# Batch 0's first stage in two halves of output rows, with the first weight halves in one software queue

## The chip, the cores and the metric

The kernel runs on one core of a Trainium2 chip. Its time is the device time of one execution in microseconds (us). The engines are TensorE (PE, with PEld for its weight loads), VectorE (DVE), ScalarE (ACT), GpSimd (POOL) and SyncE (SP, which here only issues transfers). POOL issues the transfers of the software queue, which here also turn float32 into bfloat16 on the way.

## What is computed

```
X = fft(fft(x, axis=1), axis=2).real      # x: 8 batches x 3072 x 256
h = max(X @ w1, X @ w2, X @ w3)           # 24576 x 768
out = h @ w_out                           # 24576 x 256
```

The two Fourier transforms and the weights w1, w2, w3 are real matrix products in the kernel. A row and its mirror row share products: of the two results hp and hm, the second is the first with one product more added.

## The kernel before

**The work of a batch** has three steps. Stage one (`Mix.s`, L531) has seven parts, k = 0 to 6, and multiplies the batch's x by small 96-row matrices (m24f, m24r, m0f, m0r); the seven results are copied from PSUM to the tile z. Stage two (`Mix.k`, L559) has six parts, each of eight products of z with rows of the sine table `tab`, copied to the tile t. Then come 18 units (`UNITS`, three blocks of six): `unit_plus` (L585) multiplies t by gE and gO into two PSUM tiles, pse2 and pse3; `unit_out` (L602) has ACT take relu of pse2 and DVE the maximum of that with pse3, which gives hp; `unit_minus` (L595) then adds gD to the same two tiles, and `unit_out` makes hm from them. pse2 and pse3 have two buffers each. The second matrix product (L616) and the stores follow.

**Preparation.** The gE, gO and gD tiles are made in `prep_first` (L472) from d2 = w2 - w1 and d3 = w3 - w1 (`differences`, L231), one half of the 768 columns at a time (jh = 0, 1), each by products with md, which holds the transform of the columns. Half 0 is made before the units, half 1 between units 0 and 2. `dif` and `sgn` are small per-partition constants. `prep_second` (L492) makes g1t and gw, for which w_out is needed.

**Batch 0's x** comes in four loads of rows of 128: rows 112 to 127 by SP and ACT into xs_a, and rows 0 to 39, 40 to 79 and 80 to 111 by POOL, four transfers each (L259). Each is laid out twice: in natural order (`lay_rows`, L418, tile nat) and reversed (`turn_rows`, L412, tile back), by copies that ACT and DVE share (L426 to L453). PE does warm-up products on the table until x is laid out (L772); then stage one takes nat and back whole.

**The order of the work** is written out by hand: each engine runs its instructions in the order in which the program issues them, and the list at L858 gives what is added after which unit of batch 0. So ACT's sines of table rows 10 to 12 stand in ACT's order at unit 2 (`tab_sines(10, 13, (0,))`); their angles come from POOL (`tab_angles(10, 13, nc.gpsimd)`, L793). `tab_minus` (L342) writes the negative of a part of the table.

**Queues.** POOL issues x, then both halves of w1 (L267). SP issues w2 and w3, half 0 and then half 1 (L269), after the first transfer of the third x load has landed, and behind them batch 1's x in four chunks (L458). After `first_op` (L460), which waits until x is laid out, POOL fills two constants, computes the row numbers of the stores (`store_rows`, L278, in the tiles rows_f and late of the pool `gen`), negates table rows 7 to 9 (L467), then forms the two differences of half 1, issues w_out's load, computes the angles of rows 10 to 12 and starts laying out batch 1 (`turn_chunk`, L149). The pool `gen` ends before the units begin, and later tiles take its memory.

Of the kernel before, what the change touches and what calls it, by code (L numbers as in the profile page):

```python
# [33 lines left out]
def kernel(  # L34
# [196 lines left out]
    def differences(eng, jh, which=(0, 1), after=None):  # L231
# [22 lines left out]

    pidx = gen.tile([128, 1], FP32, tag="pidx")
# [19 lines left out]
    rows_f = gen.tile([128, 7 * B], FP32, tag="rows_f")  # L275
    late = gen.tile([128, 1], FP32, tag="late")

# [145 lines left out]
    def bf_rows(r0, n):  # L423
        return x0_first[:, r0 * 64:(r0 + n) * 64]
# [20 lines left out]
    nc.scalar.activation(out=md[0], in_=vm, func=AX.Sin, scale=float(-2.0 * math.pi / 256.0))  # L445
    turn_rows(on_dve, 39, 40, 32, 65)
    lay_rows(on_act, bf_rows(40, 40), 40, 40, 12, 33)
    second_laid = lay_rows(on_dve, bf_rows(40, 40), 40, 40, 0, 12)
    for (copy, a, b, c, d) in ((on_act, 55, 64, 21, 33), (on_dve, 32, 55, 0, 21)):
        third_turned = turn_rows(copy, 79, 33, a, b)  # L450
        if copy is on_act:
            turn_rows(copy, 79, 32, 64, 65)
        laid = lay_rows(copy, bf_rows(80, 32), 80, 32, c, d)  # L453
    nc.vector.tensor_scalar(out=sgn, in0=pidx, scalar1=0.0, scalar2=None, op0=ALU.is_equal)
    nc.vector.tensor_scalar(out=sgn, in0=sgn, scalar1=2.0, scalar2=-1.0,
                            op0=ALU.mult, op1=ALU.add)
    nc.vector.tensor_scalar(out=dif, in0=sgn, scalar1=1.0, scalar2=None, op0=ALU.subtract)
    for ch in range(4):  # L458
        raw[1, ch] = load_chunk(1, ch)
    first_op = nc.gpsimd.memset(mark, 0.0)  # L460
    tc.add_manual_dep(first_op.ins, laid.ins.name, AFTER, reason="the two share a port")
    nc.gpsimd.memset(two_row, 0.0)
# [9 lines left out]
    def prep_first(jh, bank):  # L472

        cs = slice(jh * 384, (jh + 1) * 384)
        for i, wv in enumerate((d2_bf, d3_bf)):
            for half in range(2):
                psg = bank()
                hs = slice(half * 128, (half + 1) * 128)
                for fc in range(2):
                    nc.tensor.matmul(  # L480
                        psg[:, 0:384], md[fc][:, hs],
                        wv[:, fc * DFF + jh * 384: fc * DFF + jh * 384 + 384],
                        start=(fc == 0), stop=(fc == 1))
                if half == 0:
                    nc.vector.tensor_copy(out=gE[i][:, cs], in_=psg[:, 0:384])
                else:
                    nc.scalar.copy(out=gO[i][:, cs], in_=psg[:, 0:384])
                    nc.vector.tensor_scalar(out=gD[i][:, cs], in0=psg[:, 0:384], scalar1=dif,
                                            scalar2=None, op0=ALU.mult)
                yield  # L490
# [32 lines left out]
    class Mix:  # L523
# [6 lines left out]

        def s(self, k, x0, pool=ps_f, evict=nc.scalar.copy):  # L531

# [6 lines left out]
            for (d, n, mf, mr) in parts:  # L539
                if isinstance(x0, tuple):  # L540
                    pairs = ((x0[0](d), mf), (x0[1](d), mr))
                elif d:
                    pairs = ((x0[:, d, :], mf),)
                else:
                    pairs = ((x0[:, 0, :], mf), (x0[:, 33, :], mr))
                for i, (st, mv) in enumerate(pairs):
                    nc.tensor.matmul(ps1[:, c0:c0 + n], st, mv[:, 0:n], start=(i == 0),  # L547
                                     stop=(i == len(pairs) - 1))
                c0 += n
            if k < len(DLS):  # L550
                lo = 4 * DLS[k][0]
                evict(out=z[:, lo:lo + 20, 0:24],  # L552
                      in_=ps1[:, 0:480].rearrange("p (c r) -> p c r", r=24))
            else:
                evict(out=z_all[:, 0:52], in_=ps1[:, 0:52])
                evict(out=z[:, 2:8, 0:24],
                      in_=ps1[:, 52:196].rearrange("p (c r) -> p c r", r=24))

        def k(self, q, evict=nc.scalar.copy, pool=ps_f):  # L559
# [24 lines left out]

    def unit_plus(te, to, jc, n):  # L585
# [4 lines left out]
        for (pse, i) in ((pse2, 0), (pse3, 1)):  # L590
            nc.tensor.matmul(pse[:, 0:n], gE[i][:, js], te, start=True, stop=False)  # L591
# [179 lines left out]
    warm = ps_s.tile([128, 512], FP32, name="warm", tag="ps")  # L771
    for (n, after) in ((23, None), (3, second_laid), (2, third_turned)):  # L772
        for i in range(n):
            mm = nc.tensor.matmul(warm, tab[:, 0:128], tab[:, 0:512], start=True, stop=True)
# [3 lines left out]
    x0f = (lambda d: xn0[:, d, 0:128], rows_back(xr0))  # L778
    for k in range(7):
        m.s(k, x0f, pool=ps_s if k % 4 else ps_f,  # L780
            evict=nc.vector.tensor_copy if k in (1, 3) else nc.scalar.copy)
        if k == 1:
            halves = [t.rearrange("p (q two g) -> p two q g", two=2, g=4) for t in md]
            nc.vector.tensor_copy(out=halves[1][:, 0], in_=halves[0][:, 0])
            nc.vector.tensor_scalar(out=halves[1][:, 1], in0=halves[0][:, 1], scalar1=-1.0,
                                    scalar2=None, op0=ALU.mult)
            differences(nc.vector, 0, (0,))
        if k == 3:
            first_half = differences(nc.vector, 0, (1,))
            differences(nc.gpsimd, 1, after=first_half)  # L790
            nc.gpsimd.dma_start(out=wout_bf.rearrange("p (jc c) -> p jc c", jc=NJC),
                                in_=moe_w_out.rearrange("(jc p) c -> p jc c", jc=NJC))
# [100 lines left out]
    for b in range(B):  # L893
# [15 lines left out]
        for blk in range(3):  # L909
# [7 lines left out]
            for jc in range(NJC):  # L917
                pses = unit_plus(tE[:, cs], tO[:, cs], jc, TOKB)
                unit_out(pses, hp[:, jc, :], TOKB)
# [51 lines left out]
```

## Time and profile before

| what | value |
|---|---|
| median of 3 runs | 404.82 us (404.76 to 404.88) |
| the profiled execution | 404.64 us |
| its span in the profile | 402.9 us |
| instructions in the span | 8560 |
| granted TensorE clock, mean | 1.0 |

The span runs from the first to the last instruction of the profiled execution; the time of the execution includes what lies around it. In a timeline row the first number is the start in us from the begin of the span, the second the length in us, then the engine, line of the program, operation, output and inputs; in brackets is the idle time ahead of it and what ended that. In a row of the chain of waits there are start, length, engine, tile and line. In a row by stretch there are the stretch, its length, the busy time of PE, PEld, DVE, ACT and POOL with their numbers of instructions, the granted clock, the DMA share and GB/s.

### The profile page before, as it was taken

The numbers are of one execution on the slowest core, as the hardware profiler recorded it, in microseconds if no ns is written. First come the engines' busy times: TensorE is split into PE (matmuls) and PEld (weight loads), VectorE is DVE, ScalarE is ACT, GpSimd is POOL, SyncE is SP. The second block draws the span as 40 slices with busy tenths as digits, with TensorE's granted clock in tenths as the row PEclk, the third lists the DMA queues.
The fourth block names the chain that finished last, engine by engine and source line by source line (L and its number), as shares of the span: only waits on it lengthen the run. The fifth ranks groups of instructions, "written<-read, shape, count | busy, mean of one in ns | idle before, by whom it ended". The sixth has DMA issues, their size and how long they took to land.

```text
span 402.9 us, 8560 instructions
## 1 busy us (share of the span) xinstructions
PE 386.0 (96%) x2829; PEld 260.6 (65%) x2877; DVE 308.9 (77%) x556; ACT 265.5 (66%) x489; POOL 292.0 (72%) x394
## 2 busy tenths in 40 slices
PE   0999999999999999999999999999999999999996
PEld 0465667666676667666666666666677676666665
DVE  8898776788777877687776887787777877678884
ACT  6787767655866667756766677666766676655550
POOL 9599889879986998679877888768967524323521
PEclk9999999999999999999999999999999999999999
DMA  9989897789778838875478928886234411211214
GB/s 117 188 199 179 157 226 197 174 213 196 186 197 214 192 120 217 193 184 159 114 200 186 227 78 222 197 191 179 81 103 114 123 55 74 84 52 54 103 57 156
DMA packets 127597, 62.06 MB, mean 154 GB/s; under 512 B 111616, under 2 KB 116736, under 8 KB 126976
## 3 DMA queue, kind: packets, MB, share of 16 engines
q1 hardware_dynamic: 101976, 42.21, 42.3%
q0 software_dynamic: 24640, 18.98, 23.8%
q8 instruction: 22, 0.36, 0.4%
q10 hardware_dynamic: 936, 0.33, 0.3%
q14 instruction: 23, 0.19, 0.2%
HBM read 33.74 MB, written 29.88 MB: 158 GB/s over the span
## 4 chain that ended last, share of the span: by engine, by line
PE 85%; DVE 4%; DMA 3%; POOL 2%; ACT 2%; issue 2%; DVEq 0%; SPq 0%; POOLq 0%; ACTq 0%
PE po L616 29%; PE pse L591 16%; PE pse L599 14%; PE pse L592 12%; PE ps L571 3%; PE ps L573 3%; PE po L640 3%; PE pl L629 2%; PE ps L547 2%; POOL x L111 2%; DMA raw_w<-in_moe_w_dram 2%; DVE hm L606 2%; ACT stmp L605 2%; DMA x<-in_x_dram 2%; DVE other L643 1%
## 5 line engine op out<-in xcount | busy, mean ns | idle before, releaser
L605 ACT ACTIVATE stmp<-pse 128x512 bf16<-128x512 f32 x288 | 170.8, 600 | 52.6 <-PE pse L592 26.2
L606 DVE TENSOR_TENSOR hp<-pse,stmp 128x512 bf16<-128x512 f32 x144 | 99.5, 691 | 80.1 <-ACT stmp L605 51.8
L646 POOL TENSOR_TENSOR even<-even,other 128x256 f32<-128x256 f32 x92 | 70.1, 762 | 74.5 <-DVE other L643 74.2
L591 PE MATMUL pse<-t,gE 128*128 128x512 bf16 x288 | 109.1, 379 | 2.5
L606 DVE TENSOR_TENSOR hm<-pse,stmp 128x512 bf16<-128x512 f32 x144 | 99.2, 689 | 3.3 <-ACT stmp L605 3.1
L592 PE MATMUL pse<-t,gO 128*128 128x512 bf16 x249 | 94.3, 379 | 0.0
L616 PE MATMUL po<-wout_bf,hp 128*128 128x256 bf16 x576 | 85.9, 272 | 0.0
L616 PE MATMUL po<-wout_bf,hm 128*128 128x256 bf16 x570 | 85.3, 273 | 0.3
L599 PE MATMUL pse<-t,gD 128*128 128x512 bf16 x279 | 83.7, 379 | 0.1
L677 POOL DMA_INDIRECT out_dram<-ot,rows_m x53 | 53.8, 1015 | 20.2 <-DVE ot L670 10.7
L616 PEld LDWEIGHTS <-hp 128*128 128x128 bf16 x576 | 56.3, 98 | 17.3 <-issue 2.5
L616 PEld LDWEIGHTS <-hm 128*128 128x128 bf16 x576 | 56.4, 98 | 16.5
L670 DVE TENSOR_TENSOR ot<-po,even 128x512 f32<-128x512 f32 x92 | 62.8, 682 | 0.0
L173 POOL CAST xw<-xs 96x544 bf16<-96x544 f32 (+1 forms) x48 | 53.2, 1120 | 0.0
L178 POOL CAST xb<-xs 96x512 bf16<-96x512 f32 x48 | 52.4, 1100 | 0.0
L575 ACT CAST t<-ps 128x512 bf16<-128x512 f32 x48 | 27.9, 585 | 34.8 <-PE ps L573 34.7
L599 PEld LDWEIGHTS <-gD 128*128 128x128 bf16 x288 | 28.1, 98 | 32.2
L643 DVE SCALAR_TENSOR_TENSOR other<-twice,po 128x256 f32<-128x256 f32 x92 | 43.8, 476 | 0.1
L592 PEld LDWEIGHTS <-gO 128*128 128x128 bf16 x288 | 28.1, 98 | 20.4 <-issue 1.9
L591 PEld LDWEIGHTS <-gE 128*128 128x128 bf16 x288 | 28.2, 98 | 19.5 <-issue 0.7
L552 ACT CAST z_all<-ps 128x480 bf16<-128x480 f32 x46 | 24.8, 560 | 22.0 <-PE ps L547 21.9
L632 ACT COPY even<-pl 128x512 f32<-128x512 f32 x46 | 27.0, 587 | 9.7 <-PE pl L629 8.6
(178 smaller groups left out, 370.9 us busy)
## 6 DMA issues: line engine op xcount, KB each, us to landing
xs<-in_x_dram SPq DMA_DIRECT2D x84, 198.0 KB
out_dram<-ot SPq DMA_DIRECT2D x39, 256.0 KB
xs<-in_x_dram SPq DMA_DIRECT2D x28, 192.0 KB
held<-xb SPq DMA_DIRECT2D x48, 96.0 KB
xw<-held POOLq DMA_DIRECT2D x24, 192.0 KB
raw_w<-in_moe_w_dram SPq DMA_DIRECT2D x4, 384.0 KB
out_dram<-ot SPq DMA_DIRECT2D x12, 128.0 KB
x<-in_x_dram POOLq DMA_DIRECT2D x8, 120.0 KB
```

The costliest lines, as they stand in the source:

```text
L173: nc.gpsimd.tensor_copy(v[:, d0:d1, ch * 32:ch * 32 + 32], xs[:, 0:32 * 64].rearrange("p (bb dl) -> p dl bb", dl=64)[:, d0:d1, :])
L178: nc.gpsimd.tensor_copy(mir[:, d0:d1, c0:c0 + 32], bass.AP(xs.tensor, xs.offset + 33 * 64 - 1 - d0, [xs.ap[0], [-1, d1 - d0], [-64, 32]]))
L591: nc.tensor.matmul(pse[:, 0:n], gE[i][:, js], te, start=True, stop=False)
L592: nc.tensor.matmul(pse[:, 0:n], gO[i][:, js], to, start=False, stop=True)
L599: nc.tensor.matmul(pse, gD[i][:, js], to, start=False, stop=True, skip_group_check=True)
L605: nc.scalar.activation(out=stmp[:, 0:n], in_=pses[0][:, 0:n], func=AX.Relu)
L606: nc.vector.tensor_tensor(out=dst, in0=src3, in1=stmp[:, 0:n], op=ALU.max)
L616: nc.tensor.matmul(po, hcols(jc), wout_bf[:, jc * 256:(jc + 1) * 256], start=False, stop=(jc == NJC - 1), skip_group_check=True)
L643: nc.vector.scalar_tensor_tensor(out=other, in0=twice, scalar=po[:, 256:257], in1=po[:, 0:256], op0=ALU.mult, op1=ALU.subtract)
L646: nc.gpsimd.tensor_tensor(out=line[:, 256:512], in0=line[:, 0:256], in1=other, op=ALU.add)
L670: nc.vector.tensor_tensor(out=parts, in0=po.rearrange("p (i c) -> p i c", i=2), in1=lin.rearrange("p (i c) -> p i c", i=2), op=ALU.add)
L677: stored(nc.gpsimd.indirect_dma_start(out.rearrange("(n two) c -> n (two c)", two=2) if pair else out, bass.IndirectOffsetOnAxis(ap=rows_m ...
```

## The change

Stage one of batch 0 is done in two halves of z's 128 output rows. The first half (`sooner`) takes rows 0 to 63 of nat and their mirror rows of back, the second (`later`) the others; each product has 64 columns of weights and writes 64 partitions, and both halves add into seven PSUM tiles that are held at once. The copies to z follow part by part in the second half. The second x load is rows 40 to 83 and the third rows 84 to 111, so that the first half needs the first two alone. The warm-up products are 20 before the first half and one between the halves.

The first halves of w1, w3 and w2 and the second half of w1 are loaded by POOL's queue, in this order; SP loads the second halves of w3 and w2. The order of w2 and w3 is swapped in `prep_first` and in the first `unit_plus` as well. The first difference of half 0 (w3) goes from DVE to POOL, with sgn and dif. The copies within md are made before the third x load is laid out. The row numbers, pidx and late get memory that lasts (`whole`), and `store_rows` and `tab_minus(7, 10)` are issued after the differences of half 1.

```diff
+    whole = consts.tile([128, 64], FP32, tag="whole")
+    rows_f, pidx, late = whole[:, 0:7 * B], whole[:, 56:57], whole[:, 57:58]
...
-    for (r0, r1) in ((0, 40), (40, 80), (80, 112)):
+    for (r0, r1) in ((0, 40), (40, 84), (84, 112)):
...
-    for jh in range(2):
-        load_w(nc.gpsimd, w1_bf, moe_w1, jh)
-    for jh in range(2):
-        for wsrc, wdst in zip((moe_w2, moe_w3), raw_w):
-            ld = load_w(nc.sync, wdst, wsrc, jh)
-            if jh == 0:
-                tc.add_manual_dep(ld.ins, last_part[0].ins.name, AFTER, reason="x first")
+    load_w(nc.gpsimd, w1_bf, moe_w1, 0)
+    load_w(nc.gpsimd, raw_w[1], moe_w3, 0)
+    load_w(nc.gpsimd, raw_w[0], moe_w2, 0)
+    load_w(nc.gpsimd, w1_bf, moe_w1, 1)
+    for (wsrc, wdst) in ((moe_w3, raw_w[1]), (moe_w2, raw_w[0])):
+        ld = load_w(nc.sync, wdst, wsrc, 1)
+        tc.add_manual_dep(ld.ins, last_part[0].ins.name, AFTER, reason="x first")
...
-    nc.vector.tensor_scalar(out=sgn, in0=pidx, scalar1=0.0, scalar2=None, op0=ALU.is_equal)
...
+    def sooner(d):
+        return xn0[:, d, 0:64], (xr0[:, 32 - d, 64:128] if d else xr0[:, 32, 65:129])
+
+    def later(d):
+        return xn0[:, d, 64:128], (xr0[:, 32 - d, 0:64] if d else xr0[:, 32, 1:65])
...
-    nc.gpsimd.memset(two_row, 0.0)
-    nc.gpsimd.memset(two_row[0:1], 2.0)
-    nc.gpsimd.memset(gw[:, 512:513], 0.0)
-    nc.gpsimd.memset(gw[0:1, 512:513], 1.0)
-    store_rows()
-    tab_minus(7, 10, nc.gpsimd)
...
+        def s_half(self, k, rows, ps1):
+
+            begin = rows is sooner
+            if k < len(DLS):
+                parts = [(d, 96, m24f, m24r) for d in range(*DLS[k])]
+            else:
+                parts = [(0, 52, m0f, m0r), (32, 48, m24f, m24r), (1, 96, m24f, m24r)]
+            c0 = 0
+            for i, (d, n, mf, mr) in enumerate(parts):
+                for j, (st, mv) in enumerate(zip(rows(d), (mf, mr))):
+                    p0 = 64 * j if begin else 64 - 64 * j
+                    nc.tensor.matmul(ps1[p0:p0 + 64, c0:c0 + n], st, mv[:, 0:n],
+                                     start=begin and i == 0,
+                                     stop=not begin and i == len(parts) - 1,
+                                     skip_group_check=True)
+                c0 += n
...
-    for (n, after) in ((23, None), (3, second_laid), (2, third_turned)):
...
+    warm_up(20)
     m = Mix(0)
...
     for k in range(7):
-        m.s(k, x0f, pool=ps_s if k % 4 else ps_f,
-            evict=nc.vector.tensor_copy if k in (1, 3) else nc.scalar.copy)
+        m.s_half(k, sooner, banks_s[k])
+    warm_up(1, third_turned)
+    for k in range(7):
+        m.s_half(k, later, banks_s[k])
+        m.s_out(k, banks_s[k], nc.vector.tensor_copy if k % 2 else nc.scalar.copy)
         if k == 1:
...
-            differences(nc.vector, 0, (0,))
-        if k == 3:
-            first_half = differences(nc.vector, 0, (1,))
-            differences(nc.gpsimd, 1, after=first_half)
-            nc.gpsimd.dma_start(out=wout_bf.rearrange("p (jc c) -> p jc c", jc=NJC),
-                                in_=moe_w_out.rearrange("(jc p) c -> p jc c", jc=NJC))
-            tab_angles(10, 13, nc.gpsimd)
-    slots = [ps_s, ps_s, ps_f, ps_f]
+            differences(nc.gpsimd, 0, (1,))
+            nc.gpsimd.tensor_scalar(out=sgn, in0=pidx, scalar1=0.0, scalar2=None,
+                                    op0=ALU.is_equal)
...
+            nc.gpsimd.memset(two_row, 0.0)
+            nc.gpsimd.memset(two_row[0:1], 2.0)
+            nc.gpsimd.memset(gw[:, 512:513], 0.0)
+            nc.gpsimd.memset(gw[0:1, 512:513], 1.0)
+    first_half = differences(nc.vector, 0, (0,))
+    differences(nc.gpsimd, 1, (1, 0), after=first_half)
+    store_rows()
+    tab_minus(7, 10, nc.gpsimd)
+    nc.gpsimd.dma_start(out=wout_bf.rearrange("p (jc c) -> p jc c", jc=NJC),
+                        in_=moe_w_out.rearrange("(jc p) c -> p jc c", jc=NJC))
+    tab_angles(10, 13, nc.gpsimd)
+    slots = [ps_s, ps_f, ps_s, ps_f]
```

In the changed program the line numbers behind these places are up to 38 higher.

More of the change, by code (lines that the diff above doesn't have):

```diff
@@ L445 @@
     nc.scalar.activation(out=md[0], in_=vm, func=AX.Sin, scale=float(-2.0 * math.pi / 256.0))
-    turn_rows(on_dve, 39, 40, 32, 65)
-    lay_rows(on_act, bf_rows(40, 40), 40, 40, 12, 33)
-    second_laid = lay_rows(on_dve, bf_rows(40, 40), 40, 40, 0, 12)
+    turn_rows(on_dve, 39, 44, 32, 65)
+    lay_rows(on_act, bf_rows(40, 44), 40, 44, 12, 33)
+    lay_rows(on_dve, bf_rows(40, 44), 40, 44, 0, 12)
+    halves = [t.rearrange("p (q two g) -> p two q g", two=2, g=4) for t in md]
+    nc.vector.tensor_copy(out=halves[1][:, 0], in_=halves[0][:, 0])
+    nc.vector.tensor_scalar(out=halves[1][:, 1], in0=halves[0][:, 1], scalar1=-1.0,
+                            scalar2=None, op0=ALU.mult)
     for (copy, a, b, c, d) in ((on_act, 55, 64, 21, 33), (on_dve, 32, 55, 0, 21)):
-        third_turned = turn_rows(copy, 79, 33, a, b)
+        third_turned = turn_rows(copy, 83, 29, a, b)
         if copy is on_act:
[L452 to L457, printed above, removed]
+            turn_rows(copy, 83, 28, 64, 65)
+        laid = lay_rows(copy, bf_rows(84, 28), 84, 28, c, d)
+    def sooner(d):
+        return xn0[:, d, 0:64], (xr0[:, 32 - d, 64:128] if d else xr0[:, 32, 65:129])
+    def later(d):
+        return xn0[:, d, 64:128], (xr0[:, 32 - d, 0:64] if d else xr0[:, 32, 1:65])
     for ch in range(4):
@@ L487, in prep_first @@
                     nc.scalar.copy(out=gO[i][:, cs], in_=psg[:, 0:384])
-                    nc.vector.tensor_scalar(out=gD[i][:, cs], in0=psg[:, 0:384], scalar1=dif,
-                                            scalar2=None, op0=ALU.mult)
+                    scaled.append((gD[i][:, cs], psg[:, 0:384]))
+                if half and (jh or not i):
+                    for (dst, product) in scaled:
+                        nc.vector.tensor_scalar(out=dst, in0=product, scalar1=dif,
+                                                scalar2=None, op0=ALU.mult)
+                    scaled = []
                 yield
```

28 lines of the change are left out of this document (15 added, 13 removed).

## The prediction

> **What bounds the kernel now.** I read the page from the top first: busy time, then the chain that ended last.
>
> ```profile
> span 402.9 us, 8560 instructions
> PE 386.0 (96%) x2829; PEld 260.6 (65%) x2877; DVE 308.9 (77%) x556; ACT 265.5 (66%) x489; POOL 292.0 (72%) x394
> ...
> PE 85%; DVE 4%; DMA 3%; POOL 2%; ACT 2%; issue 2%; DVEq 0%; SPq 0%; POOLq 0%; ACTq 0%
> ```
>
> PE is busy for 96% of the span and holds 85% of the chain. Then the busy time by stretch, to see where PE is not the limit:
>
> ```profile
> 0.00:18.67 18.67, 8.33 (x29) 3.12 (x29) 15.87 (x58) 14.31 (x23) 13.55 (x22) 1.00 1.73 137
> ...
> 24.18:33.18 9.00, 8.70 (x47) 4.75 (x48) 8.01 (x15) 7.93 (x16) 8.80 (x8) 1.00 0.91 164
> ...
> 40.00:400.00 360.00, 356.98 (x2633) 244.18 (x2676) 274.83 (x466) 234.21 (x432) 258.28 (x350) 1.00 0.60 152
> ```
>
> From 40 to 400 us PE lacks 3 us of being always busy, so a delay that PE enters that stretch with is not made up there: what happens before 40 us reaches the end one for one, up or down. Up to 18.67 PE's work is only warm-up. Between 24.18 and 33.18 POOL is busy 8.80 of 9.00 us: POOL, not PE, is the fullest engine there. The chain of waits says the same:
>
> ```profile
> 2.63 6.14 POOL x L111 x7
> 8.76 6.22 DMA x<-in_x_dram
> ...
> 15.98 7.10 DMA raw_w<-in_moe_w_dram
> ...
> 23.25 1.65 POOL d_bf L233
> ...
> 31.98 0.45 PE pst L499 x4
> ...
> 33.18 0.38 PE pse L591
> 33.56 0.22 PE pse L592
> ```
>
> So batch 0's x, then the weights w2 and w3, then POOL's differences set the start.
>
> **The change, part by part.** First stage one. The timeline of PE, then of DVE, ACT:
>
> ```profile
> 10.01 7.73 PE L774 MATMUL warm<-tab 128*128 128x512 bf16 x26 [10.01 <-DVE tab L343]
> ...
> 18.67 0.20 PE L547 MATMUL ps<-m24f,nat 96*128 96x96 bf16 x1
> 18.71 0.20 PE L547 MATMUL ps<-m24r,back 96*128 96x96 bf16 x1
> ...
> 21.36 0.20 PE L547 MATMUL ps<-m24r,back 96*128 96x96 bf16 x1
> ...
> 14.23 1.33 DVE L144 COPY back<-x 96x1320 bf16<-96x1320 bf16 x1
> 15.48 0.58 DVE L419 COPY nat<-x 96x480 bf16<-96x480 bf16 x1
> 17.03 0.83 DVE L144 COPY back<-x 96x759 bf16<-96x759 bf16 x1 [0.97 <-DMA x<-in_x_dram]
> 17.78 0.74 DVE L419 COPY nat<-x 96x672 bf16<-96x672 bf16 x1
> ...
> 17.77 0.85 ACT L419 COPY nat<-x 96x384 bf16<-96x384 bf16 x1
> 21.99 0.31 ACT L556 CAST z_all<-ps 128x144 bf16<-128x144 f32 x1
> ```
>
> The first half of stage one needs rows 0 to 63, that is the first two loads. The second load grows from 40 to 44 rows, so DVE's two copies of it grow by 1.1: 14.23 + 1.25 x 1.1 + 0.58 x 1.1 = 16.25; with an estimated 0.3 us by which a load with a tenth more in it lands later, 16.55. The third shrinks to 28 or 29 rows: 17.03 + 0.75 x 0.88 + 0.65 = 18.35, and ACT's share ends near 18.45. So the second half can begin at 18.4, where all of stage one began at 18.67.
>
> What a half costs is not in the trace. Stage one's 66 matmuls now start about 0.042 us apart, the first at 18.67 and the last at 21.36: 2.7 us. A half has 66 too, each writing 64 partitions instead of 128. If two neighbours, which write different partitions, run beside each other, a half takes 1.4; if not, 2.7. No row is nearer to one than to the other; I take 2.1, and keep both ends. The Trainium skill, TensorEngine Tiling (Array Packing), "Theoretical Speedup", has two-way column tiling up to twice as fast, which would be the 1.4; its "Restrictions" say that column tiling switches off fast weight load, which speaks against this change; no run here shows either, and the sum below does not hang on it.
>
> With 2.1 the first half is 16.55 to 18.65, the one warm-up 0.22, the second half 18.9 to 21.0, and z is copied out by about 21.6 (DVE now takes three of seven copies, ACT four), where it was 22.30. With 1.4 it is 20.9. The copies of md move into DVE's idle 0.97 us ahead of 17.03 and cost nothing there (without that cover 0.2 us). sgn and dif leave DVE, the first d3 difference too. Fewer warm-ups cost nothing: 20 of them end before 16.55.
>
> Now the weights and POOL. POOL's timeline:
>
> ```profile
> 12.94 1.48 POOL L263 DMA_DIRECT2D w_bf<-in_moe_w_dram  x2
> 18.59 0.09 POOL L460 MEMSET mark<- 1x1 f32 x1 [4.17 <-DVE sgn L454]
> 18.62 0.20 POOL L462 MEMSET two_row<- 128x128 bf16 x1
> ...
> 19.22 0.45 POOL L245 IOTA rows_f<- 128x40 f32 x3
> 19.75 0.27 POOL L283 TENSOR_SCALAR late<-pidx 128x1 f32<-128x1 f32 x1
> 20.11 0.35 POOL L285 TENSOR_SCALAR rows_f<-rows_f,late 128x8 f32<-128x8 f32 x1
> ...
> 21.52 1.19 POOL L343 TENSOR_SCALAR tab<-tab 128x384 bf16<-128x384 bf16 x1
> 23.25 3.24 POOL L233 TENSOR_TENSOR d_bf<-raw_w,w_bf 128x768 bf16<-128x768 f32 x2 [0.54 <-DMA raw_w<-in_moe_w_dram]
> 26.44 0.91 POOL L791 DMA_DIRECT2D wout_bf<-in_moe_w_out_dram  x1
> 27.37 0.85 POOL L319 TENSOR_TENSOR w_late<-pi_all,step 128x384 f32<-128x384 f32 x1
> ...
> 29.57 1.00 POOL L329 TENSOR_TENSOR w_late<-w_high,w_late 128x384 f32<-128x384 f32 x1
> 30.52 2.04 POOL L158 CAST x<-xs 96x1056 bf16<-96x1056 f32 x1
> ```
>
> Two more weight loads are issued by POOL, 0.74 us each: 14.42 becomes 15.9, inside POOL's 4.17 us of idle time ahead of the mark, so nothing. SP issues two fewer, so batch 1's chunks start about 1 us sooner behind them.
>
> Before, POOL laid out the row numbers (19.22 to 21.52, 2.30 us) and tab_minus (to 22.75, 1.23 us) **while it waited** for w2 and w3. The change puts both behind the two second-half differences, and puts in their place the first d3 difference (1.64), three tiny operations for sgn and dif (0.36 each by the starts at 19.75 and 20.11, 1.1) and the four memsets (0.6). From the mark at 18.4 these end at 21.8. That is the earliest for the second-half differences; the latest is their start of before, 23.25, since the same six loads share the same engines. Which load lands last in the new order no row shows (w1's second half is now the last of its queue); I take the middle, 22.5. Then:
>
> 22.5 + 3.2 (both differences) + 2.30 + 1.23 + 0.93 (w_out's issue) + 3.2 (the angles of rows 10 to 12, 27.37 to 30.57) = 33.35, where it was 30.57. With the bounds: 32.65 to 34.1.
>
> Who waits for these angles? ACT's sines of rows 10 to 12, in unit 2 of batch 0, whose place in ACT's order is unchanged:
>
> ```profile
> 30.24 0.59 ACT L575 CAST t<-ps 128x512 bf16<-128x512 f32 x1
> 30.72 0.53 ACT L335 ACTIVATE tab<-w_late 128x384 bf16<-128x384 f32 x1
> 31.15 1.26 ACT L605 ACTIVATE stmp<-pse 128x512 bf16<-128x512 f32 x2
> ...
> 31.77 0.69 DVE L606 TENSOR_TENSOR hp<-pse,stmp 128x512 bf16<-128x512 f32 x1 [0.26 <-PE pse L599]
> 32.44 0.69 DVE L606 TENSOR_TENSOR hm<-pse,stmp 128x512 bf16<-128x512 f32 x1
> ```
>
> Before, the angles were ready at 30.57 and ACT came to them at 30.72: it just fitted. Now ACT comes about 0.9 us sooner (first differences of the second half done at 22.5 + 1.6 = 24.1 instead of 24.90, and z sooner) and **stands until 33.4**. Queued behind the sine on ACT are unit 3's two outputs (31.15), behind them DVE's two (31.77, 32.44), and behind those PE's unit 4 at 33.18, as the buffers come free only then. So PE's 33.18 becomes 33.18 + (33.45 - 30.72) = 35.9: **2.75 us later**, whatever was gained ahead of it; POOL's chunk of batch 1 moves from 30.52 to 33.3, the same amount, so nothing catches up. d3's first difference starts no later than POOL's chain allows and adds nothing more.
>
> w_out is issued 2.8 us later, and PE's use of it moves as far: nothing. d2's difference on DVE ends by about 22.6, beside 22.5 on POOL. The swapped order of w3 and w2, the later gD and the other banks only shift work within the gain that ACT then waits away: nothing, with at most 0.3 either way. Row numbers in memory of their own take no time; they let the row numbers be written late.
>
> Sum: 404.64 us (the profiled execution: span 402.9 and 1.7 around it; 0.2 under the median of 404.82) + 2.75 = **407.4**. Bounds by POOL's start alone: +2.1 to +3.5, 406.7 to 408.1.
>
> **The rivals.**
>
> 1. The gain of stage one reaches the end (403.7). Mechanism: POOL's row numbers and tab_minus shrink, because at 19 to 22 us they ran beside DVE's differences, and the angles are done when ACT arrives. Price: -0.9. It decides only if POOL ends them by 29.8, 3.5 us sooner than worked out. Against: the operations from 18.4 on add up to 32.65 with no wait at all. For: spans on POOL are rough.
>
> 2. Halves one matmul at a time: 2.7 each. First half to 19.25, second 19.5 to 22.2, z at 22.75, DVE's difference of d2 at 23.7, for which POOL's second-half differences wait: 1.2 us behind 22.5, so 408.6. The turning point is a half of 2.1 us. For: the matmuls of 18.67 start one after another; against: they all write the same partitions.
>
> 3. The clock falls. PE's last work ahead of unit 4 ended at 32.43 and would end near 31.5; unit 4's first buffer comes free when ACT's pair at 31.15 has ended, 32.41 + 2.75 = 35.15: a pause of 3.6 us. The first 26 warm-ups took 7.73 us, where 26 at the 0.22 of the row at 33.56 take 5.7: a cold start costs 2.0 us. If the pause were long enough, 409.4. Against: the stretches above all have the clock at 1.00; for: none of them has a pause like it. The Trainium skill, TensorE: Matmul & The Clock Gate, "Why this matters for your kernels" counts gaps of over about 3 us between bursts of matmuls as enough to go back to half clock; the pause worked out here stands just above it, and no run here yet has such a gap.
>
> 4. The change doesn't do what it says: the one queue brings w1's second half later than 23.25, for instance at 24.2. Then every microsecond of it comes on top: 408.5.
>
> **How the numbers follow.** Forecast (406.4 to 408.1) 0.58; rival 1 0.12; rival 2 0.07; rival 3 0.10; rival 4 0.06; a pause partly taken back by PE, within 0.2% (what a measurement of this kernel can tell from no change), 0.05; slower by less than the forecast's low end 0.02. The range 405.6 to 409.6 leaves out rival 1, the unchanged case (0.17 together) and little above. Faster 0.12, same 0.05, slower 0.83.
>
> **What would show it.** In the changed profile: (a) stage one's matmuls begin near 16.55, z's last copy ends before 22; (b) POOL's second-half differences begin between 21.8 and 23.25 and the angles end near 33.3; (c) ACT's sine after unit 2 shows an idle time of 3 to 4 us ended by POOL's w_late; (d) PE has one gap of 3 to 4 us there, and the rest of the run is the old one, 2.7 us later; (e) the clock stays at 1.00. The forecast is wrong if (c) shows no wait: then rival 1. It is too low if the first-half matmuls stay 0.042 apart for 2.7 us, or the clock row drops behind the gap.

## The result, and the profile after

| | before | changed |
|---|---|---|
| median, us | 404.79 (404.41 to 405.21, 6 executions) | 410.40 (407.98 to 410.95, 6 executions) |
| ratio | | 1.0131 (95% interval 1.0106 to 1.0156) |
| profiled execution, us | 404.64 | 410.13 |
| its span, us | 402.9 | 408.3 |
| granted clock, mean | 1.0 | 0.996 |

The change costs 5.6 us. The forecast was 407.4 with a range up to 409.6: the sign was right, the size half of what came. Five executions had a granted clock of 0.996 and took 410.11 to 410.95 us; the one at 1.0 took 407.98.

The page of the changed kernel: span, busy time, shares of the chain that ended last.

```profile
span 408.3 us, 8675 instructions
...
PE 385.6 (94%) x2887; PEld 260.6 (64%) x2936; DVE 308.2 (75%) x553; ACT 265.1 (65%) x488; POOL 295.9 (72%) x400
...
PE 83%; DVE 5%; POOL 4%; ACT 3%; issue 2%; DMA 2%; DVEq 0%; ACTq 0%; POOLq 0%
```

PE is as busy as before (386.0 us then) in a span that is 5.4 us longer, so it waits more; POOL and ACT have gained shares of the chain. The same stretches as in the prediction, and the one between, show where (after each engine's busy time come the clock, the share of the DMA engines and GB/s):

```profile
24.18:33.18 9.00, 7.33 (x43) 4.17 (x42) 5.97 (x10) 5.25 (x10) 8.50 (x14) 1.00 0.87 170
33.18:40.00 6.82, 3.92 (x15) 2.29 (x16) 3.27 (x5) 4.19 (x8) 6.82 (x5) 0.76 0.91 165
40.00:400.00 360.00, 356.98 (x2619) 242.94 (x2664) 275.86 (x468) 237.49 (x438) 262.27 (x352) 1.00 0.59 150
```

From 40 to 400 us PE is busy for 356.98 us, as before. Nearly all of the loss is made by 40 us: PE loses 1.37 us of work between 24.18 and 33.18, and in the 6.82 us behind that it works for 3.92 (6.60 before), part of them at half clock. Now the steps, in order. Stage one's first half, its end, the second half (PE), and the last copies of z (ACT, DVE):

```profile
16.71 0.23 PE L578 MATMUL ps<-m24f,nat 96*64 96x96 bf16 x1 [1.05 <-DVE nat L417]
16.72 0.23 PE L578 MATMUL ps<-m24r,back 96*64 96x96 bf16 x1
...
18.08 0.21 PE L578 MATMUL ps<-m24r,back 96*64 96x96 bf16 x1
18.54 0.23 PE L578 MATMUL ps<-m24f,nat 96*64 96x96 bf16 x1 [0.25 <-issue]
...
19.90 0.21 PE L578 MATMUL ps<-m24r,back 96*64 96x96 bf16 x1
...
20.43 0.32 ACT L564 CAST z_all<-ps 128x144 bf16<-128x144 f32 x1
```

The two matmuls of a pair start 0.00 to 0.01 us apart, the pairs 0.042: a half takes 1.37 us from its first start to its last, and z is out by 21 us instead of 22.3. This part did what it says. The Trainium skill, TensorEngine Tiling (Array Packing), "Theoretical Speedup", has two column tiles up to twice as fast; the trace agrees, as 66 products of half the width take 1.37 us instead of 2.7. Its "Restrictions" name the loss of fast weight load; what that costs, no run here shows by itself.

POOL, and the transfers that were issued between 14 and 24.5 us (the last number is the time from issue to landing):

```profile
18.39 1.65 POOL L233 TENSOR_TENSOR d_bf<-raw_w,w_bf 128x768 bf16<-128x768 f32 x1
...
21.32 0.09 POOL L824 MEMSET gw<- 1x1 bf16 x1
23.85 3.24 POOL L233 TENSOR_TENSOR d_bf<-raw_w,w_bf 128x768 bf16<-128x768 f32 x2 [2.44 <-DVE gD L491]
27.05 0.46 POOL L247 IOTA whole<- 128x40 f32 x3
27.58 0.24 POOL L281 TENSOR_SCALAR whole<-whole 128x1 f32<-128x1 f32 x1
...
28.54 0.23 POOL L286 CAST rows_m<-whole 128x56 int32<-128x56 f32 x1
28.74 1.20 POOL L341 TENSOR_SCALAR tab<-tab 128x384 bf16<-128x384 bf16 x1
...
33.04 0.99 POOL L327 TENSOR_TENSOR w_late<-w_high,w_late 128x384 f32<-128x384 f32 x1
```

```profile
w_bf<-in_moe_w_dram POOLq DMA_DIRECT2D x1, 192.0 KB, 8.7
```

POOL is done with its small work at 21.4 and then stands for 2.44 us. The row names a DVE operation, which ended at 23.65 by the chain of waits, but the transfer of w1's second half, issued at 15.00, took 8.7 us to land: 23.7. It is the fourth weight load in its queue. The DVE operation that the program makes POOL wait for, d2's difference, had ended by 21.9, so the transfer is what is left; run 10's trace names it. Then the chain runs without a break and the angles end at 34.03. ACT's sine, and PE's units around it:

```profile
25.54 0.81 PE L480 MATMUL psg<-d_bf,md_all 128*128 128x384 bf16 x4 [1.33 <-POOL d_bf L233]
...
34.07 0.52 ACT L333 ACTIVATE tab<-w_late 128x384 bf16<-128x384 f32 x1 [2.74 <-POOL w_late L327]
...
35.61 0.38 PE L616 MATMUL pse<-t,gE 128*128 128x512 bf16 x1 [2.69 <-ACT stmp L630]
...
40.73 0.38 PE L616 MATMUL pse<-t,gE 128*128 128x512 bf16 x1
```

ACT stands for 2.74 us, PE for 2.69: the wait that was forecast, in its place and nearly in its size. What was not in the sum comes behind it. From unit 4's first product to unit 5's takes 5.12 us here (35.61 to 40.73) and took 3.34 before, 1.78 less. The rows of before for the first product of unit 4 and of unit 5 (the prediction's row at 33.18 is unit 4's second pair, into pse3):

```profile
32.45 0.38 PE L591 MATMUL pse<-t,gE 128*128 128x512 bf16 x1
...
35.79 0.38 PE L591 MATMUL pse<-t,gE 128*128 128x512 bf16 x1
```

So unit 4 begins 3.16 us later than before and unit 5 4.94 us later. Two stretches of the changed kernel, each 3.41 us long, show why:

```profile
33.26:36.67 3.41, 0.81 (x4) 0.29 (x4) 1.56 (x3) 2.57 (x6) 3.41 (x3) 1.00 1.14 187
36.67:40.08 3.41, 3.19 (x14) 2.02 (x14) 1.71 (x3) 1.62 (x3) 3.41 (x3) 0.50 0.66 144
```

PE worked for 0.81 of the 3.41 us that hold the pause, and for the next 3.41 us its clock is at half. At half clock PE does in 3.41 us what otherwise takes 1.71, so such a stretch by itself costs at most about 1.7 us (an estimate from these two numbers).

### The profile page after: what moved, and what is told of

The parts are those of the page before. It is cut to its first block, busy times and chain, and to the rows that moved or that the text cites. A ratio compares the mean times of both kernels' runs of the same rounds, so it can differ in the third digit from the quotient of the medians.

```text
span 408.3 us, 8675 instructions
## 1 busy us (share of the span) xinstructions
PE 385.6 (94%) x2887; PEld 260.6 (64%) x2936; DVE 308.2 (75%) x553; ACT 265.1 (65%) x488; POOL 295.9 (72%) x400
## 3 DMA queue, kind: packets, MB, share of 16 engines
q0 software_dynamic: 24864, 19.77, 23.7%
## 4 chain that ended last, share of the span: by engine, by line
PE 83%; DVE 5%; POOL 4%; ACT 3%; issue 2%; DMA 2%; DVEq 0%; ACTq 0%; POOLq 0%
PE po L641 28%; PE pse L616 15%; PE pse L624 14%; PE pse L617 12%; PE ps L596 3%; PE ps L598 3%; PE po L665 2%; PE pl L654 2%; ACT stmp L630 2%; DVE hm L631 2%; PE ps L551 2%; POOL x L111 2%; DMA x<-in_x_dram 2%; DVE other L668 1%; POOL d_bf L233 1%
## 5 line engine op out<-in xcount | busy, mean ns | idle before, releaser
L630 ACT ACTIVATE stmp<-pse 128x512 bf16<-128x512 f32 x288 | 170.7, 600 | 54.7 <-PE pse L617 34.1
L702 POOL DMA_INDIRECT out_dram<-ot,rows_m x53 | 54.0, 1020 | 19.9 <-DVE ot L695 10.7
```

What stands on the lines that cost most here:

```text
L630: nc.scalar.activation(out=stmp[:, 0:n], in_=pses[0][:, 0:n], func=AX.Relu)
L702: stored(nc.gpsimd.indirect_dma_start(out.rearrange("(n two) c -> n (two c)", two=2) if pair else out, bass.IndirectOffsetOnAxis(ap=rows_m ...
```

## The experiments

Theory A: four links. POOL's new order brings the angles late; w1's second half as fourth load of the queue brings the differences late; PE's pause costs its own length; and the pause then costs a second time, by the clock. Rivals put the loss into the halves of stage one themselves, into the queue alone, or take the clock to be a bystander.

**1. POOL's order alone** (in the kernel before, with the row numbers in memory of their own):

```
-    store_rows()
-    tab_minus(7, 10, nc.gpsimd)
...
             differences(nc.gpsimd, 1, after=first_half)
+            store_rows()
+            tab_minus(7, 10, nc.gpsimd)
```

> The kernel before with one thing moved: the row numbers (in memory that lasts) and table rows 7 to 9 are issued on POOL behind the second-half differences, as in the changed kernel. Theory A: differences from 23.25 to 26.44, then 1.7 to 2.3 for the row numbers, 1.2, 0.95 and 3.2: the angles end at 33.5 to 34.1, ACT's sine idles some 2.8 to 3.4 us; 407.5 without and about 409.9 with a fall of the clock. Theory B: 404.8, no change.

Measured: 409.85 us (408.60 to 411.64, 5 executions, all at a clock of 0.996), ratio 1.0140 (1.0116 to 1.0163). ACT's sine, the first products of PE's units 4 and 5, and the stretches of 3.41 us:

```profile
33.38 0.52 ACT L334 ACTIVATE tab<-w_late 128x384 bf16<-128x384 f32 x1 [2.38 <-POOL w_late L328]
...
34.92 0.38 PE L588 MATMUL pse<-t,gE 128*128 128x512 bf16 x1 [2.33 <-ACT stmp L602]
...
39.74 0.38 PE L588 MATMUL pse<-t,gE 128*128 128x512 bf16 x1
```

```profile
31.76:35.18 3.42, 1.09 (x8) 0.62 (x7) 0.76 (x2) 1.80 (x4) 3.34 (x3) 1.00 1.12 154
35.18:38.59 3.41, 3.37 (x12) 1.54 (x11) 2.51 (x4) 1.87 (x5) 3.41 (x4) 0.50 0.85 148
```

The unit begins 2.47 us later than before. Two moved calls bring 5.0 of the 5.6 us, with the same wait, pause and fall. Stage one and the queue are as before here.

**2. The same, with the pause filled** by products that nobody reads, ahead of unit 4:

```
+    def fill():
+        bank = ps_f.tile([128, 512], FP32, name="bank", tag="ps")
+        for _ in range(12):
+            nc.tensor.matmul(bank, tab[:, 0:128], tab[:, 0:512], start=True, stop=True)
...
-    (3, prep_some), (3, lambda: tab_sines(10, 13, (1, 2))),
+    (3, prep_some), (3, fill), (3, lambda: tab_sines(10, 13, (1, 2))),
```

> The kernel before with POOL's new order alone (409.85 us, every execution at a granted clock of 0.996), and 12 matmuls whose result nobody reads put into PE's queue ahead of the unit that waits for ACT's sine. They need 2.6 us at full rate and stand in a pause of 2.3 us. Theory A (the pause costs twice: its own length, and then 3.4 us at half rate, since PE was busy for only 1.09 us of the 3.41 us before): granted clock 1.0 in all executions, 407.2 to 408.2 us. Theory B (the fall of the clock belongs to a busy POOL and ACT, not to PE's pause): clock 0.996 as before, 409.5 us or more.

Measured: 407.29 us (406.91 to 407.88), every execution at 1.0.

```profile
31.96 2.75 PE L855 MATMUL bank<-tab 128*128 128x512 bf16 x12
34.83 0.38 PE L588 MATMUL pse<-t,gE 128*128 128x512 bf16 x1
...
38.43 0.38 PE L588 MATMUL pse<-t,gE 128*128 128x512 bf16 x1
```

```profile
31.47:34.89 3.42, 3.30 (x18) 1.62 (x17) 0.57 (x1) 1.61 (x4) 3.34 (x3) 1.00 1.15 162
```

ACT and POOL are about as busy as in run 1 and unit 4 comes no sooner (34.83 instead of 34.92 us); only PE is not idle. The clock stays. So the fall follows from PE's pause. Its price is less sure than its cause. The medians differ by 409.85 - 407.29 = 2.56 us, which is more than the 1.7 that a half-rate stretch can cost by itself. The executions of run 1 lie 3 us apart at the same clock, and the profiled one, 408.60, is the fastest of them. In the two traces unit 4's first product to unit 5's takes 4.82 us in run 1 and 3.60 here: 1.2 us, and the two profiled executions differ by 1.3. What makes the other executions of run 1 slower isn't shown. What is left of run 1, 2.5 us, is the wait (unit 4 at 34.83 instead of 32.45).

**3. The changed kernel with its pause filled** (the same `fill`):

```
-    (3, prep_some), (3, lambda: tab_sines(10, 13, (1, 2))),
+    (3, prep_some), (3, fill), (3, lambda: tab_sines(10, 13, (1, 2))),
```

> The changed kernel with twelve more warm-up products on PE ahead of unit 4, 2.6 us of work that nothing reads, inside the pause of 35.61 - 32.98 = 2.6 us. Theory A with the clock as a second cost: ACT's wait of 2.7 us stays, the clock stays at 1.00, and every run is near the one run of the changed kernel without the fall, 408.0. If the pause alone is the whole cost and the fall of the clock is harmless: 410.4 as before, in spite of a clock of 1.00.

Measured: 409.49 us (407.60 to 410.85), ratio 1.0114 (1.0089 to 1.0139); five of six executions at 0.999 or 1.0. That is between the two numbers expected, 408.0 and 410.4. The clock was kept in the pause, yet the median fell by only 0.9. In the profiled execution (409.34) POOL's differences began at 25.00 us instead of 23.85 and PE stood 2.6 us in all for differences, so that unit 4 came 1.16 us later than in the changed kernel. From there its trace can be compared:

```profile
36.77 0.38 PE L616 MATMUL pse<-t,gE 128*128 128x512 bf16 x1
...
40.22 0.38 PE L616 MATMUL pse<-t,gE 128*128 128x512 bf16 x1
```

From unit 4 to unit 5 it takes 3.45 us, where the changed kernel takes 5.12. That prices the fall at 1.67 us; with run 2, at 1.2 to 1.7.

**4. The loads alone** (in the kernel before):

```
-    for jh in range(2):
-        load_w(nc.gpsimd, w1_bf, moe_w1, jh)
...
+    load_w(nc.gpsimd, w1_bf, moe_w1, 0)
+    load_w(nc.gpsimd, raw_w[1], moe_w3, 0)
+    load_w(nc.gpsimd, raw_w[0], moe_w2, 0)
+    load_w(nc.gpsimd, w1_bf, moe_w1, 1)
+    for (wsrc, wdst) in ((moe_w3, raw_w[1]), (moe_w2, raw_w[0])):
...
```

> The kernel before with the new order of the weight loads alone: first halves of w1, w3, w2 and then w1's second half by the software queue, the second halves of w3 and w2 by SP's. Theory A (w1's second half lands last, at 23 to 24.5 us, and POOL's second-half differences wait for it instead of for SP's): they start 0.3 to 1.3 us later than the 23.25 us of before, PE waits up to 0.7 us more near 26 us, and the angles end at 31 to 32 us, still ahead of ACT; 404.9 to 406 us. Theory B (the order of the loads does nothing): 404.5 to 405.1 us with the start at 23.0 to 23.5 us.

Measured: 406.25 us (406.08 to 407.55), ratio 1.0043 (1.0028 to 1.0058).

```profile
24.84 3.24 POOL L233 TENSOR_TENSOR d_bf<-raw_w,w_bf 128x768 bf16<-128x768 f32 x2 [1.67 <-DVE gE L485]
...
26.53 0.81 PE L480 MATMUL psg<-d_bf,md_all 128*128 128x384 bf16 x4 [0.88 <-POOL d_bf L233]
```

The differences start 1.6 us later than before (23.25) and PE waits 0.88 us for them: the new queue order loses 1.5 us by itself, a little more than theory A had. One of the six executions (407.55) had a fall of the clock.

**5. The halves alone** (the kernel before, with `s_half`, the 44-row load, the changed warm-ups and the copies to z as in the changed kernel; weight loads and POOL's order as before; DVE's two differences of half 0 come behind stage one instead of within it):

```
-        m.s(k, x0f, pool=ps_s if k % 4 else ps_f,
...
+        m.s_half(k, sooner, banks_s[k])
+    warm_up(1, third_turned)
...
+        m.s_half(k, later, banks_s[k])
```

> The kernel before with stage one in halves (rows 40 to 83 and 84 to 111, warm-ups, copies of md, copies to z as in the changed kernel), but the weights' loads, the differences and POOL's order of before. Theory A: no wait at ACT's sine, so no loss: z is complete near 20.9 instead of 22.3, but the first products with d2 wait for its difference (20.9 + 0.95), and POOL's differences of the second half start at 23.25 as before, so little is gained: 404.2 to 405.0. If the halves themselves cost time (narrow products, a drain): 405.5 or more.

Measured: 406.15 us (404.52 to 406.96, 12 executions), ratio 1.0029 (1.0013 to 1.0044). Missed: no gain, but a loss of 1.3 us. At a clock of 0.999 or 1.0, 404.52 to 406.44 us in seven executions (median 405.17); at 0.994 to 0.996, 406.50 to 406.96 in five. So without a fall the halves are 0.3 us behind the kernel before (404.83), with one 1.8. The profiled one (404.99) shows where the sooner z goes (DVE, then PE):

```profile
20.68 1.88 DVE L233 TENSOR_TENSOR d_bf<-raw_w,w_bf 128x768 bf16<-128x768 f32 x2
...
21.75 0.82 PE L491 MATMUL psg<-d_bf,md_all 128*128 128x384 bf16 x4 [1.85 <-DVE d_bf L233]
```

PE is done with stage one at 19.9 us and then waits 1.85 us for d2's difference. DVE begins that at 20.68, right behind its copies to z and with no wait for w2; before, it began at 20.49, between two such copies.

**6. The halves with more warm-ups** (run 5, with):

```
-    warm_up(20)
+    warm_up(23)
...
+    warm_up(3)
     warm_up(1, third_turned)
```

> The kernel before with the two halves alone (loads and POOL's order as before), and the same 23 and 4 warm-up matmuls. The halves alone gave 406.15 us, with a granted clock of 0.994 to 0.996 in 5 of 12 executions at 406.5 to 407.0 us and 1.0 in the others at 404.5 to 406.4 us. If PE's pauses around the halves bring these falls: clocks of 0.999 or 1.0 throughout and 404.5 to 405.2 us. If not: clocks mixed as before, about 406.2 us.

Measured: 406.31 us (405.98 to 407.36). Missed: three of seven executions still at 0.996 (407.17 to 407.36), and the others, at 405.98 to 406.31, slower than the median of 405.17 of run 5's. In the profiled execution the pauses around the halves were filled, the one of 1.80 us for d2 was not, and DVE's difference began at 21.66 us, 1 us later than in run 5.

**7. The angles first** (the changed kernel):

```
-    store_rows()
-    tab_minus(7, 10, nc.gpsimd)
     nc.gpsimd.dma_start(out=wout_bf.rearrange("p (jc c) -> p jc c", jc=NJC),
...
     tab_angles(10, 13, nc.gpsimd)
+    tab_minus(7, 10, nc.gpsimd)
+    store_rows()
```

> The changed kernel with one thing moved: POOL issues w_out and the angles of rows 10 to 12 right behind the second-half differences, and table rows 7 to 9 and the row numbers after them. Theory A (ACT's sine of rows 10 to 12 stands until POOL's angles come, and the clock falls in the pause): the angles end near 27.05 + 0.95 + 3.2 = 31.2, just when ACT comes to its sine (31.3), no idle time there, no pause of PE, clock 1.00, time 404.8 to 405.5, as the second-half differences still start 0.6 us later than before (23.85 against 23.25). Theory B (the loss comes from the loads: w1's second half is the last of its queue and lands at about 23.7): no more than some tenths come back, 408 or more.

Measured: 407.52 us (406.62 to 408.75), ratio 1.0078 (1.0059 to 1.0097). ACT's sine no longer waits and unit 4 has no pause: 2.9 us back, but 2 us short of theory A. In the profiled execution the clock fell elsewhere:

```profile
16.25:19.66 3.41, 1.94 (x73) 1.66 (x75) 3.01 (x6) 2.68 (x4) 1.16 (x3) 1.00 1.10 355
19.66:23.08 3.42, 3.42 (x69) 2.88 (x68) 2.27 (x4) 2.06 (x5) 2.64 (x8) 0.50 1.09 262
```

PE stood 2.03 us ahead of the first half there, until x was laid out at 17.72, and the second half ran at half clock. That execution took 407.01 us. The other five had no fall (406.62 to 408.75), so something else was left: the next runs.

**8. w1's second half third in the queue** (the changed kernel, w2's first half back on SP's queue, first of three):

```
     load_w(nc.gpsimd, raw_w[1], moe_w3, 0)
-    load_w(nc.gpsimd, raw_w[0], moe_w2, 0)
     load_w(nc.gpsimd, w1_bf, moe_w1, 1)
-    for (wsrc, wdst) in ((moe_w3, raw_w[1]), (moe_w2, raw_w[0])):
-        ld = load_w(nc.sync, wdst, wsrc, 1)
+    for (wsrc, wdst, jh) in ((moe_w2, raw_w[0], 0), (moe_w3, raw_w[1], 1), (moe_w2, raw_w[0], 1)):
+        ld = load_w(nc.sync, wdst, wsrc, jh)
```

> The changed kernel with one load moved: w2's first half goes back to SP's queue, first of three there, so that w1's second half is third instead of fourth in the software queue; POOL's order stays. Theory A (the fourth place sets POOL's start at 23.85 us, and with it the 1.33 us that PE waits at 25.54 us and part of the wait for the angles): w1's second half lands by about 21 to 22 us, POOL's second-half differences start at 22.0 to 23.0 us, PE's wait near 25.5 us is under 0.7 us, the angles end at 32.2 to 33.2 us, ACT's sine still waits 1 to 2 us; 407 to 408.5 us, 2 to 3 us less than the changed kernel. Theory B (the queue is innocent, the second halves on SP's queue set the start anyway): start stays at 23.5 us or later, 410 us or more.

Measured: 408.50 us (407.16 to 411.00), ratio 1.0106 (1.0078 to 1.0134). In the profiled execution (407.16) the differences start at 22.89 us and PE's wait of 1.33 us for them is gone (one of 1.16 us for the first differences stands at 20.84), but ACT and PE then come to the late angles sooner, and the pause is as long as ever:

```profile
34.65 0.38 PE L615 MATMUL pse<-t,gE 128*128 128x512 bf16 x1 [2.69 <-ACT stmp L629]
```

Four of six executions fell to 0.995 or 0.996, the profiled one did not. The median is 1.9 us below the changed kernel's, though the pause stayed; the two intervals overlap.

**9. Both** (the edits of runs 7 and 8 together):

> The same load order, and POOL's order as in the run with the angles first. Theory A (what is left of the loss in that run, 407.52 us, is PE's wait for the second-half differences): 404.8 to 405.8 us, with no wait of PE over 0.5 us between 22 and 40 us. Theory B (what is left comes from the two halves of stage one themselves, or from the clock early on): 406.5 to 408 us, as with the angles first alone.

Measured: 406.12 us (405.51 to 407.48, 12 executions), ratio 1.0033 (1.0020 to 1.0046), all at 0.999 or 1.0. That is between the two theories' numbers: 1.4 us below run 7, so the queue's place was about half of what run 7 had left; 1.3 us stay. DVE at 48 us:

```profile
47.97 0.69 DVE L694 TENSOR_TENSOR ot<-po,even 128x512 f32<-128x512 f32 x1 [1.46 <-POOL even L670]
```

PE waits for this operation until 48.72, 1.47 us. POOL has had no break since 23.18 us, and the row numbers that it now makes at 31.64 us are 1.7 us that batch 1's casts and this sum come later. The loss had moved down POOL's queue.

**10. Run 9 with 23 and 4 warm-ups** (the edit of run 6):

> The same as the last, with 23 warm-up matmuls instead of 20 ahead of the first half and 4 instead of 1 between the halves, so that no stretch of 3.4 us in stage one holds an idle PE for over about 1 us. If the clock falls early in some executions because PE pauses around the first half (as the profile of the run with the angles first shows, half rate from 19.66 to 23.08 us), all executions here have a granted clock of 0.999 or 1.0 and the median is 0.3 to 1.2 us below the run before: 404.2 to 405.0 us. If the early falls have another cause, the clocks stay mixed and the median stays.

Measured: 406.87 us (406.37 to 407.34), ratio 1.0049. Missed: run 9 had no falls to lose, and the median is 0.7 us above run 9's, with overlapping intervals. One row is of use, since here the trace names the transfer that POOL's differences wait for:

```profile
22.91 3.29 POOL L233 TENSOR_TENSOR d_bf<-raw_w,w_bf 128x768 bf16<-128x768 f32 x2 [1.52 <-DMA w_bf<-in_moe_w_dram]
```

**11. The changed kernel with the row numbers in POOL's gap** (one line moved):

```
+    store_rows()
     first_half = differences(nc.vector, 0, (0,))
     differences(nc.gpsimd, 1, (1, 0), after=first_half)
-    store_rows()
```

> The changed kernel with one line moved: the row numbers are made ahead of the second-half differences, in the gap from 21.4 to 23.85 us in which POOL waits for w1's second half. Theory A: the differences still start within 0.3 us of when w1's second half lands, the angles end 1.4 to 1.7 us earlier (32.4 to 32.7 us), ACT's sine still waits about 1.0 to 1.3 us and PE about 1 us, under what lets the clock fall in most executions; 407 to 408.3 us against 410.4. Theory B (the queue's fourth place and the clock alone make the loss): 409.5 us or more.

Measured: 407.09 us (406.38 to 407.72), ratio 1.0058 (1.0044 to 1.0073), all at 0.998 to 1.0.

```profile
33.00 0.52 ACT L333 ACTIVATE tab<-w_late 128x384 bf16<-128x384 f32 x1 [1.07 <-POOL w_late L327]
...
34.54 0.38 PE L616 MATMUL pse<-t,gE 128*128 128x512 bf16 x1 [1.02 <-ACT stmp L630]
```

One line gives back 3.3 of the 5.6 us. ACT's wait and PE's pause shrink by 1.7 us, and no execution has the fall.

**12. Run 9 with the row numbers in the gap:**

```
+    store_rows()
     first_half = differences(nc.vector, 0, (0,))
...
     tab_minus(7, 10, nc.gpsimd)
-    store_rows()
```

> The kernel with w1's second half third and the angles first, and the row numbers made in POOL's idle gap ahead of the second-half differences. There (406.12 us) POOL runs without a break from 23.18 us to beyond 48 us, and PE waits 1.47 us at 48.72 us for a tile of layer two whose even half POOL adds after all its casts. Theory A (what is left of the loss is POOL's 1.69 us of row numbers, put behind the differences instead of into a gap in which POOL waits for weights): the wait at 48.7 us falls to under 0.4 us, the differences start no more than 0.4 us later; 404.6 to 405.3 us. Theory B (the halves themselves lose it): 405.8 us or more.

Measured: 405.69 us (404.72 to 407.39, 12 executions), ratio 1.0021 (1.0009 to 1.0032). Between the two theories' numbers: 0.4 us better than run 9, still 0.9 over the kernel before. In the profiled execution, the slowest of the twelve, the wait at 48.7 us is gone, but the differences start at 24.40 us and PE stands 1.64 us for them at 26.09, after which the clock falls. The gap was too short there: POOL came to the row numbers only at 22.71 us and was busy until the differences, which in run 9 had begun at 23.18. No run here beats the kernel before.

## Why the prediction was wrong

Point by point, by its own steps:

- **Stage one**: begins at 16.71 (forecast 16.55), a half takes 1.4 us (2.1 taken, with 1.4 as one end). Right within its bounds, and worth nothing, as it said; alone it is worth nothing either, in run 5 it even costs 1.3 us, mostly by falls of the clock.
- **POOL's chain**: the second-half differences start at 23.85, outside the bounds of 21.8 to 23.25 and 1.35 us over the 22.5 taken. The reason for the upper bound, that the same six loads share the same engines, did not hold; rival 4 had it right. The row numbers took 1.69 us (27.05 to 28.74) instead of 2.30. So the angles end at 34.03 instead of 33.35, within 34.1. The shorter row numbers are what rival 1 counted on (`tab_minus` did not shrink), but the angles came late all the same.
- **ACT's wait**: there, 2.74 us instead of 3 to 4: PE had waited 1.33 us for the late differences and ACT came later.
- **PE's delay: a term that was too small.** ACT's sine begins at 34.07 instead of 30.72, 3.35 us later, where 33.45 - 30.72 = 2.73 was taken, since the angles came 0.7 us later than summed. Unit 4's first product, in rows of one kind, moves from 32.45 to 35.61: 3.16 us, where the sum has 2.75 (it compared with 33.18, the unit's second pair, which moves by 3.27 to 36.45). With 3.16 the sum gives 407.8; the one execution without a fall took 407.98.
- **The clock: the step that failed.** The forecast worked out a pause of 3.6 us and then let the clock's fall be a rival of its own, at 0.10, although it was this forecast's own pause that would bring it; in the sum the fall stands at nothing. The reason given against it, that all stretches of before have a clock of 1.00, said nothing, as none of them has such a pause. Five of six executions fell. From unit 4 to unit 5 PE takes 1.78 us more than before (5.12 instead of 3.34), of which 1.67 go when the pause is filled (run 3): 404.64 + 3.16 + 1.78 = 409.6. The profiled execution took 410.13; the last 0.5 us come behind unit 5 and were not followed.
- **Rival 3** had the right cause and came nearest with 409.4, partly by luck: its price of 2.0 us, taken from the warm-ups, is above the 1.2 to 1.7 of the traces, its delay of 2.75 below the 3.16 measured.
- **The page of the Trainium skill** that was weighed there (TensorE: Matmul & The Clock Gate, "Why this matters for your kernels") counts gaps of over about 3 us. Here a pause of 2.69 us was enough in the changed kernel's profiled execution and one of 2.33 in run 1's, all of whose five executions fell. The pause worked out, 3.6 us, lay above the page's figure as well, and the fall was still given only 0.10.

By parts: POOL's order alone costs 5.0 us, the loads 1.5, the halves 1.3. The sum of 7.8 is more than the 5.6 of the whole. Run 8 shows one way in which the parts cover one another: when PE's wait of 1.33 us for the differences goes, PE comes to the angles sooner and its pause there stays as long.

## What to carry to other kernels

When a sum moves a pause onto the matmul engine, price the pause twice, once for its length and once for the clock behind it (here up to 1.7 us), and look at how much of each 3.41 us the engine works, not at the pause alone. Before moving work out of a gap, ask whether the gap stays: here POOL still stood for 2.44 us of waiting for weights, while the 1.7 us of row numbers that had filled it ran later, on the path to the end. A stage that is made faster gains only what the next input allows: here d2's difference, which stood behind DVE's copies to z (run 5), and w1's landing.

## What the runs showed of the hardware

**The clock goes by fixed stretches.** In all profiles the half-rate spells in mid-run last 3.41 us, and begin a whole number of such stretches after the clock's rise: risen at 12.84 in run 7, fallen at 19.66 (2 x 3.41 later) by the trace's records of the clock, and so in the changed kernel and in runs 1 and 12 (7, 6 and 4 stretches). The Trainium skill, TensorE: Matmul & The Clock Gate, "What's actually happening", has a free-running window of 3413 ns; the trace agrees. It lets the clock fall after an idle window; here windows in which PE was busy for 0.81 us (changed), 1.09 (run 1), 1.94 (run 7) and 1.45 were enough, the last in run 12:

```profile
22.98:26.39 3.41, 1.45 (x7) 0.60 (x7) 2.12 (x4) 1.20 (x3) 3.10 (x8) 1.00 0.80 137
26.39:29.80 3.41, 3.41 (x11) 1.37 (x9) 1.87 (x3) 1.85 (x4) 3.30 (x4) 0.50 0.81 168
```

But in runs 6 and 9 such windows passed without a fall:

```profile
20.76:24.17 3.41, 1.61 (x19) 1.30 (x13) 3.32 (x6) 1.40 (x5) 1.43 (x2) 1.00 0.96 221
```

```profile
46.51:49.92 3.41, 1.95 (x15) 1.30 (x14) 1.95 (x4) 1.62 (x3) 3.22 (x5) 1.00 0.99 184
```

So in these profiles the clock fell behind every window below 1.5 us, and of those from 1.6 to 2 us only behind run 7's, whose busy time is mostly the 64-column products of stage one; whether that is why was not tried. Busy time alone does not give the threshold; what does stays open.

Where the pause lies in the windows matters. Run 8's profiled execution has a pause of 2.69 us at unit 4 like the changed kernel's, but it is split over two windows, and the clock stayed:

```profile
30.32:33.73 3.41, 1.64 (x10) 0.78 (x9) 0.72 (x2) 0.67 (x3) 3.23 (x4) 1.00 1.26 181
33.73:37.15 3.42, 2.21 (x13) 1.38 (x14) 2.77 (x5) 3.14 (x7) 3.42 (x3) 1.00 0.94 177
```

The windows' place shifts from profile to profile (the clock rises at 12.38 us in run 9 and at 14.70 in run 1). That would explain why some kernels had both kinds of executions; it was not tried.

**A small POOL operation waits out DVE's difference.** In run 11 the 1-column operation at L281 takes 0.91 us and ends at 23.10, just behind DVE's difference at 23.00 (0.24 us without it, at 27.58 in the changed kernel). DVE's row and POOL's:

```profile
22.04 0.96 DVE L233 TENSOR_TENSOR d_bf<-raw_w,w_bf 128x768 bf16<-128x768 f32 x1 [1.37 <-DMA raw_w<-in_moe_w_dram]
...
22.19 0.91 POOL L281 TENSOR_SCALAR whole<-whole 128x1 f32<-128x1 f32 x1
```

So it was with the row numbers before, whose last cast took 0.81 us before and takes 0.23 in the changed kernel: that is the 0.6 us by which they shrank when moved. The row of before:

```profile
20.73 0.81 POOL L288 CAST rows_m<-rows_f 128x56 int32<-128x56 f32 x1
```

The Trainium skill, GPSIMD Engine Reference, "1. Specifications", has POOL share its SBUF interfaces with DVE, with contention beside DVE instructions that have two SBUF inputs, as the difference has; these rows agree.
